# A small transpose moved from the DMA crossbar to TensorE, with a new order of all operations

## Chip, cores and metric

One core of one Trainium2 chip. The metric is the device time of one execution in microseconds (us). For this program on one core a run is called slow when it is over 1.5% above the fastest run of the same kernel, and fast otherwise. Most such slow runs of the kernel before show the same granted clock as its fast ones (of 53 executions on five chips, from 316.2 to 335.8 us, all but four lie between 0.98 and 1.00), so the label marks how the run went, and the figures don't show another state of the chip. (They say little about the start: the clock records of these profiles begin only at 13.8 to 56.1 us, and what lies before the first record is counted as full clock.) Of the 53 executions 21 are fast (316.2 to 322.0 us, with a mean of 318.1 to 319.2 in each of the five groups) and 32 slow (321.5 to 335.8, means 326.3 to 328.7). I give two ratios for each experiment: of the fast runs, and of the means of all runs.

## The reference

Linear attention with a feature map for 8 batches and 8 heads, then a gated long convolution on its output. Cut to what matters:

```python
def phi(x):                                  # q and k: (8, 8, 576, 64)
    proj = einsum('bhsd,df->bhsf', x, w_phi)             # 128 features
    proj = proj - max(abs(proj), axis=-1, keepdims=True) # row maxima
    return concatenate([exp(proj), exp(-proj)], axis=-1)
num = phi(q) @ (phi(k)^T v);  den = phi(q) @ sum_s phi(k)
x = num / (den + 1e-6)                       # -> (8, 576, 512)
x1, x2, x3 = split(x @ w_proj, 3)
y = x1 * irfft(rfft(x2) * rfft(filter)) * x3 # over the sequence, by DFT matrices
out = y @ w_out
```

## The kernel before

The whole kernel is one list of words, the PLAN. Each word calls a method that emits one operation; an engine runs its operations in the order of the list, and so does a queue of DMA issues. GpSimd issues the loads from DRAM (it casts on the way), SyncE issues the filter loads and all transposing transfers through the DMA crossbar.

```python
for word in PLAN.split():                    # run(): "Pq,0,1@2" -> self.Pq(0, 1) in PSUM bank 2
    name, _, bank = word.partition("@")
    self.bank = int(bank) if bank else None
    f, *args = name.split(",")
    getattr(self, f)(*[int(a) if a.isdigit() else a for a in args])

def load(self, n, b):                        # q, k or v of batch b: 576 KB, GpSimd's queue
    self.nc.gpsimd.dma_start(out=self.at(n + "n", b)..., in_=self.dram[n][b]...)

def trh(self, n, b, X):                      # half a batch: qT or kT, crossbar, SyncE's queue
    self.nc.sync.dma_start_transpose(
        out=self.at(n + "T", b)[:, 9 * X:9 * X + 9, :],
        in_=self.at(n + "n", b)[:, 2 * X:2 * X + 2].rearrange("p v j d -> p (v j d)"))

def gen_fwd(self):                           # the DFT matrix; gen_fwd5 is its second part
    self.nc.sync.dma_start_transpose(out=self.at("fwd")..., in_=self.G...)

def trm(self, b):                            # row maxima of q as two bf16 parts, 128x128
    self.nc.sync.dma_start_transpose(
        out=self.at("mT", b), in_=self.at("mh", b).rearrange("p g h x -> p (g h x)"))
# ... cut: w_load (w_proj in three parts of 512 KB, GpSimd), filt_load (nine loads, SyncE),
# trx, trxt (xT, xTt by the crossbar, SyncE), Pq (features of q transposed, minus mT through
# a selecting matmul), X1, X2, X3 (the projections with w_proj), H, F (DFT of filter and x2) ...
```

## Time and profile before

| | us |
|---|---|
| median of the three timed runs | 327.88 |
| lowest to highest of them | 326.14 to 329.03 |
| span of the core in the profile, an execution of 318.73 us | 317.0 |

In the lines of the profile PE is TensorE, PEld its weight load, DVE VectorE, ACT ScalarE, POOL GpSimd and SP SyncE; a q behind the name means that the engine's sequencer issues or waits, and L684 is a line of the kernel.

### The profile page before, as it was taken

The numbers are of one execution on the slowest core, as the hardware profiler recorded it, in microseconds if no ns is written. First come the engines' busy times: TensorE is split into PE (matmuls) and PEld (weight loads), VectorE is DVE, ScalarE is ACT, GpSimd is POOL, SyncE is SP. The second block draws the span as 40 slices with busy tenths as digits, with TensorE's granted clock in tenths as the row PEclk, the third lists the DMA queues.
The fourth block names the chain that finished last, engine by engine and source line by source line (L and its number), as shares of the span: only waits on it lengthen the run. The fifth ranks groups of instructions, "written<-read, shape, count | busy, mean of one in ns | idle before, by whom it ended". The sixth has DMA issues, their size and how long they took to land.

```text
span 317.0 us, 9411 instructions
## 1 busy us (share of the span) xinstructions
PE 278.9 (88%) x3901; PEld 161.2 (51%) x3901; DVE 250.7 (79%) x415; ACT 230.4 (73%) x363; POOL 220.5 (70%) x171
## 2 busy tenths in 40 slices
PE   0653478899999999999799999999999999999991
PEld 0433265546675556466355545654565554654440
DVE  6994459999988888888689898987898866786750
ACT  4794378989888888886778867788768877635542
POOL 8697914799988786698589868956688566813230
PEclk9955559999999999999999999999999999999998
DMA  6999995899889996999979949565338311360346
GB/s 123 239 211 186 223 218 82 125 155 166 143 125 179 174 144 110 205 71 132 217 147 147 164 70 205 103 116 136 78 54 125 82 35 25 70 118 2 78 95 159
DMA packets 78666, 41.50 MB, mean 131 GB/s; under 512 B 58976, under 2 KB 73440, under 8 KB 78624
## 3 DMA queue, kind: packets, MB, share of 16 engines
q1 hardware_dynamic: 63808, 24.66, 45.4%
q0 software_dynamic: 14816, 16.25, 34.6%
q8 instruction: 30, 0.49, 0.6%
q14 instruction: 12, 0.10, 0.1%
HBM read 33.75 MB, written 9.44 MB: 136 GB/s over the span
## 4 chain that ended last, share of the span: by engine, by line
PE 70%; DVE 11%; DMA 8%; ACT 3%; POOL 3%; issue 2%; SPq 1%; POOLq 0%; DVEq 0%; ACTq 0%
PE ps L844 16%; PE ps L801 9%; PE ps L895 8%; PE ps L936 8%; PE ps L458 5%; DMA out_dram<-o 5%; PE ps L709 5%; PE ps L730 4%; DMA kT<-kn 3%; DVE mq L654 3%; PE ps L587 2%; PE ps L851 2%; PE ps L594 2%; PE ps L615 2%; PE ps L621 2%
## 5 line engine op out<-in xcount | busy, mean ns | idle before, releaser
L844 PE MATMUL ps<-xT,wproj 128*128 128x512 bf16 x256 | 64.1, 379 | 0.2 <-DVE mq L654 0.2
L913 POOL TENSOR_TENSOR yT<-cv,x1s 128x576 bf16<-128x576 f32 x27 | 34.3, 1279 | 31.2 <-DVE cv L903 14.0
L654 DVE TENSOR_REDUCE mq<-ps 128x8 f32<-128x1024 f32 (+1 forms) x40 | 43.8, 1111 | 7.7 <-PE ps L594 6.7
L654 DVE TENSOR_REDUCE mk<-ps 128x8 f32<-128x1024 f32 (+1 forms) x40 | 44.2, 1112 | 3.6 <-PE ps L587 1.4
L694 POOL TENSOR_TENSOR vp<-vn,vp 128x1152 bf16<-128x1152 bf16 x16 | 34.5, 2154 | 9.2 <-ACT vp L688 7.1
L638 ACT ACTIVATE Ekm<-ps 128x1024 bf16<-128x1024 f32 x32 | 32.6, 1026 | 9.7 <-PE ps L587 5.9
L694 POOL TENSOR_TENSOR vm<-vn,vm 128x1152 bf16<-128x1152 bf16 x16 | 34.4, 2151 | 7.3 <-ACT vm L688 7.3
L936 PE MATMUL ps<-wout,yT 128*128 128x512 bf16 x144 | 36.2, 379 | 0.1
L638 ACT ACTIVATE Eqm<-ps 128x1024 bf16<-128x1024 f32 x32 | 32.7, 1025 | 4.9 <-PE ps L621 4.7
L832 POOL TENSOR_TENSOR t<-C,B 128x1024 bf16<-128x1024 bf16 x13 | 27.5, 2120 | 12.5 <-ACT C L714 9.4
L895 PE MATMUL ps<-inv,Y 128*128 128x288 bf16 (+1 forms) x192 | 36.0, 289 | 0.0
L638 ACT ACTIVATE Ekp<-ps 128x1024 bf16<-128x1024 f32 x32 | 32.9, 1028 | 3.7 <-DVE mk L654 2.2
L638 ACT ACTIVATE Eqp<-ps 128x1024 bf16<-128x1024 f32 x32 | 32.7, 1025 | 3.5 <-PE ps L621 2.8
L844 PEld LDWEIGHTS <-wproj 128*128 128x128 bf16 x256 | 23.1, 98 | 23.1 <-issue 0.2
L801 PE MATMUL ps<-wproj,eo 128*128 128x512 bf16 x128 | 31.1, 379 | 0.6 <-DVE KVs L716 0.6
L903 DVE TENSOR_TENSOR cv<-es,ps 128x288 f32<-128x288 f32 x64 | 26.5, 448 | 6.0 <-PE ps L895 4.1
L837 POOL TENSOR_TENSOR Y<-Y,t 128x1024 bf16<-128x1024 bf16 x14 | 29.6, 2125 | 2.3 <-DVE Y L827 1.1
L827 DVE TENSOR_TENSOR Y<-ps,A 128x1024 bf16<-128x1024 f32 (+1 forms) x24 | 24.7, 1042 | 4.6 <-PE ps L458 2.1
L714 ACT COPY o<-ps 128x512 f32<-128x512 f32 x29 | 17.0, 591 | 12.3 <-PE ps L936 7.6
L881 DVE TENSOR_TENSOR x1s<-ps,x1s 128x512 bf16<-128x512 f32 x32 | 21.7, 686 | 5.1 <-PE ps L844 4.7
L895 PEld LDWEIGHTS <-Y 128*128 128x128 bf16 (+1 forms) x192 | 14.4, 96 | 18.3 <-issue 9.7
L714 ACT CAST x1s<-ps 128x512 bf16<-128x512 f32 (+1 forms) x30 | 16.6, 552 | 9.6 <-PE ps L844 7.9
(153 smaller groups left out, 635.3 us busy)
## 6 DMA issues: line engine op xcount, KB each, us to landing
out_dram<-o SPq DMA_DIRECT2D x72, 128.0 KB, 2.4
vn<-in_v_dram POOLq DMA_DIRECT2D x8, 576.0 KB, 9.9
kn<-in_k_dram POOLq DMA_DIRECT2D x7, 576.0 KB, 10.0
qn<-in_q_dram POOLq DMA_DIRECT2D x7, 576.0 KB, 8.6
wproj<-in_moe_w_proj_dram POOLq DMA_DIRECT2D x3, 512.0 KB, 9.2
fl<-in_moe_filter_fft_dram SPq DMA_DIRECT2D x18, 64.0 KB, 5.0
kn<-in_k_dram POOLq DMA_DIRECT2D x2, 288.0 KB, 5.8
qn<-in_q_dram POOLq DMA_DIRECT2D x2, 288.0 KB, 8.1
```

Of the source, the lines that this page charges most:

```text
L638: self.nc.scalar.activation(e, self.db(), AF.Exp, bias=0.0, scale=1.0 if g == "p" else -1.0)
L654: self.nc.vector.tensor_reduce(out=out, in_=src, axis=AX.X, op=ALU.max, apply_absolute_value=True)
L694: self.port(eng, self.elem(eng).tensor_tensor(out=t[:, :, :, 0:64], in0=self.at("vn", b)[:, 2 * X:2 * X + 2], in1=t[:, :, :, 64:65].to_bro ...
L714: self.nc.scalar.copy(dst, src)
L801: self.mm(self.pb(0), eo[:, kt, 128 * c:128 * c + 128], w[:, kt, 512:1024], start=(kt == 0), stop=(kt == 3))
L832: self.port(eng, self.elem(eng).tensor_tensor(out=self.at("t2", b)[:, t, :], in0=self.at("C", b)[:, o, :], in1=self.at("B"), op=ALU.mult))
L837: self.port(eng, self.elem(eng).tensor_tensor(out=Y, in0=Y, in1=self.at("t2", b)[:, i:i + 3:2, :], op=ALU.add if i else ALU.subtract))
L844: self.mm(self.pb(0), w[:, kt, f0 + 128 * m:f0 + 128 * m + 128], x[:, kt, :], start=(kt == 0), stop=(kt == 3))
L895: self.mm(self.pb(0, 0, 288), y, t, start=(k == 0), stop=(k == 2))
L903: self.nc.vector.tensor_tensor(out=self.at("cv", 4 * b + m)[:, :, odd, :], in0=e, in1=o, op=ALU.subtract if odd else ALU.add)
L913: self.port(eng, self.elem(eng).tensor_tensor(out=self.at("yT", b)[:, m, 0:SEQ], in0=self.at("cv", 4 * b + m).rearrange("p j h t -> p (j h ...
L936: self.mm(self.pb(0), y[:, kt, 128 * j:128 * j + 128], w[:, kt, :], start=first and kt == ks[0], stop=last and kt == ks[-1])
```

## The change

The intent: take eight crossbar transfers out of a shared in-order queue, let TensorE transpose the 128x128 tile with the identity matrix it already has, copy it out of PSUM, and order all operations anew around that. The operations proper:

```diff
-    def trm(self, b):
-        self.nc.sync.dma_start_transpose(
-            out=self.at("mT", b), in_=self.at("mh", b).rearrange("p g h x -> p (g h x)"))
+    def Tm(self, b):
+        self.nc.tensor.transpose(self.turned(1), self.at("mh", b).rearrange("p g h x -> p (g h x)"),
+                                 self.at("ident"))
+    def Tme(self, eng, b):
+        self.copy(eng, self.at("mT", b), self.turned(1))
```

The rest of the diff is the PLAN, of which every line changes. Cut to the DMA issues between the first loads and the first projection X1 of batch 0, with marks where work of PE stands:

```
before: load v0 | nine fl | load k1 | load q1 | nine fl | trh k1,0 | trh q1,1 | trh q1,0 |
        w_proj 1 | trm 0 | (Pq 0) | fwd | trh k1,1 | fwd5 | load k2 | trh k2,1 | trh k2,0 | trx 0,0 |
        load v1 | trx 0,1 | w_proj 0 | trx 0,3 | load q2 | trm 1 | trx 0,2 | trxt 0 | load q3 |
        trh q2,0 | w_proj 2 | (X1 0) ... trh q2,1 | load k3 ... load v2
after:  load q1 | load k1 | nine fl | trh q1,0 | trh q1,1 | trh k1,0 | nine fl | load v0 | trh k1,1 |
        fwd | fwd5 | load k2 | (Tm 0, Pq 0) | trh k2,1 | trh k2,0 | w_proj 0 | trx 0,0 | trx 0,1 |
        load q2 | trh q2,0 | trh q2,1 | load v1 | trx 0,3 | w_proj 2 | trx 0,2 | w_proj 1 | trxt 0 |
        load k3 | load v2 | trx 1,0 | trh k3,1 | (X1 0) ...
```

Load and w_proj issues stand on GpSimd's queue, all others on SyncE's. Besides this some copies change engines.

## The prediction

> **What bounds the kernel now.** The core ran 317.0 us in the profile, with a mean granted TensorE clock of 0.947, in the fast state; the timed runs have a median of 327.88 us. I take the difference of some 10 us between profiled and timed runs as constant and work in profile time. I read first the page's shares and slices, to see which engine is full and where.
>
> ```profile
> PE 278.9 (88%) x3901; PEld 161.2 (51%) x3901; DVE 250.7 (79%) x415; ACT 230.4 (73%) x363; POOL 220.5 (70%) x171
> ...
> PE   0653478899999999999799999999999999999991
> ...
> PEclk9955559999999999999999999999999999999998
> ```
>
> PE is the fullest engine, but 88% is an average of two stages: slices 0 to 6 are poor, from slice 8 on all but one are full. Second, the busy times in three stretches, columns PE, PEld, DVE, ACT, POOL, clock, DMA share, GB/s.
>
> ```profile
> 0.00:60.00 60.00, 31.24 (x558) 22.94 (x558) 44.38 (x85) 40.46 (x59) 40.50 (x49) 0.74 1.01 177
> 60.00:310.00 250.00, 247.31 (x3344) 138.25 (x3343) 206.31 (x331) 188.73 (x303) 180.04 (x123) 1.00 0.76 119
> 310.00:317.00 7.00, 0.38 (x2) 0.00 (x0) 0.00 (x0) 1.17 (x2) 0.00 (x0) 0.80 0.65 151
> ```
>
> PE is idle 28.8 us before 60 us, 2.7 us in the 250 us after it, and 6.6 us in the tail. So a better order can win nearly nothing in the middle; what is to be had is at the start, and perhaps a microsecond in the tail. Third, the waits of PE, to see what the start waits for (microseconds, times, longest).
>
> ```profile
> PE ps L568 <- DMA kn<-in_k_dram: 10.1, 1, 10.1
> PE ps L587 <- DMA kT<-kn: 4.9, 1, 4.9
> PE ps L594 <- DMA qT<-qn: 4.7, 1, 4.7
> PE ps L568 <- ACT Ekp L638: 1.7, 1, 1.7
> PE ps L601 <- DMA kT<-kn: 1.4, 1, 1.4
> ...
> PE ps L621 <- DMA mT<-mh: 0.5, 1, 0.5
> ```
>
> The first 10.1 us are the first load and stay. Then come the crossbar transposes of batch 1 (kT, qT). The transfer that the change removes (mT) shows only 0.5 us. That figure hides its lateness, because an in-order engine is charged only for the wait that ends last. The SyncE queue of the start shows it (start, length, instruction).
>
> ```profile
> 20.59 1.34 SPq L548 DMA_TRANSPOSE kT<-kn  x1
> 23.43 8.37 SPq L548 DMA_TRANSPOSE qT<-qn  x2
> 31.89 1.18 SPq L683 DMA_TRANSPOSE mT<-mh  x1
> 33.17 2.16 SPq L400 DMA_TRANSPOSE fwd<-G  x1
> 35.38 3.80 SPq L548 DMA_TRANSPOSE kT<-kn  x1
> ```
>
> The source mh of batch 0 is done at 26.4 us (the timeline of VectorE: 26.19 plus 0.20). Its transfer stands in the queue behind two qT transposes and is issued at 31.89, and the first matmul that reads mT starts at 38.06. That is 11.7 us for a tile of 32 KB. Likewise the second half of kT of batch 1 is issued at 35.38 and lands 8.94 us later, a piece of the chain of waits by itself. Between 20 and 50 us VectorE is busy for 17.55 us of 30, ScalarE for 17.07: 12.5 us of VectorE time are lost there.
>
> **What the Trainium skill says.** (1) "TensorE: Matmul & The Clock Gate", Part 1: a TensorE that is not kept busy runs at half clock, and full clock comes after a few microseconds of sustained work. The trace agrees: granted clock 0.50 from 20 to 40 us, and eight Pk matmuls take 0.61 us there against 0.40 at 50.73. (2) The same page, Part 4: a PE-mode transpose of 128x128 bf16 takes about 275 ns in a kernel and lands in PSUM, so a copy follows. The trace has 18 of them from qn at a mean of 293 ns, at a part of which the clock was half. (3) "DMA: Bandwidth & Descriptors", section "Issuing engines are not separate DMA queues": all DMAs interleave on the same 16 engines. The trace agrees: mT lands 2.2 us after issue at best, 3.4 in the median and 7.6 at worst, and the DMA share between 20 and 50 us is 1.22. (4) "Perfetto Trace Analysis", "Identifying the Most-Contended Engine": matmul busy share is no good measure of the distance to the peak. I therefore checked the middle by spacing: four 512-column matmuls take 0.86 us in the chain, 0.216 each, and summing all groups at such spacings gives by my estimate about 243 us of array work in the 250. So even with hidden bubbles the middle holds perhaps 7 us, and a new order will not get all of that.
>
> **The change, part by part.** I counted both lists of operations. They are the same but for eight trm, which become eight Tm and eight Tme (5 on VectorE, 3 on ScalarE), and for the engines of some copies and products.
> - *Removed:* eight crossbar transfers, 1.18 us each of the SyncE queue, 9.4 us in all, none on the path in the middle: there PE never waited for mT. At the start the one of batch 0 cost the delay above.
> - *Added:* eight transposes on PE. At full clock one occupies the array for about 0.06 us (four 128-column matmuls in the time of a 512-column one, 0.216/4), so 0.5 us in all, on the bounding engine. Eight small copies: 0.215 us on VectorE (the row of 128x128 copies to qT), 0.27 to 0.30 on ScalarE, some 1.9 us in all, hidden in the middle.
> - *Engines moved:* weighting the moved copies and products by their rows, VectorE gains 4.5 us (with its Tme), GpSimd loses 3.2, ScalarE stays. VectorE was 83% busy in the middle and would be 84%: not a bound.
> - *New order of the start.* q comes first, q and k of batch 1 are loaded before v of batch 0, their transposes go ahead of the fwd ones, and Tm of batch 0 stands right behind its maxima. I walked the in-order lists of the start with the durations of the trace. VectorE: the angle work ends at 12.6 us as before; then copies of kT and qT, five maxq, one maxk and small work bring mlo to about 20.7, and Tme of batch 0 comes at about 24.7. So Pq of batch 0 can start at 25 in place of 36.9. Going on through batch 1 (ten maxima, 1.22 us or 0.68 each), the xn, the five filter evictions and the two folds, VectorE reaches the first X1 and X2 evictions at about 51 us if it never waits; ScalarE's walk gives 52, GpSimd's vs and filter folds let NE of batch 1 go at 48. Before, the first X1 matmul is at 60.9 us. About the same PE work precedes it in both lists, so time saved up to there is time saved at the end: at most some 10 us.
> - *Waits that stay:* the loads share the DMA engines as before, and a crossbar transpose landed 7 to 10 us after issue in that stretch. The kT of batch 1, second half, stands behind nine filter loads in the new queue; I expect it at 36 to 38 us, about when its matmuls are due. I give 3.5 us of the 10 back for that and for dependent chains at half clock (the KV group took 2.1 us there, against 1.15 later).
>
> Sum: -10 + 3.5 at the start, +0.5 for transposes, -1 to +2 in middle and tail, taken as -0.5: about -6.5 to -7, so 310.2 in the profile and about 321 timed.
>
> **The rivals.** *The wait moves.* Loads stay the limit of the start (the DMA engines move 199 GB/s from 20 to 50 us at a share of 1.22), and PE then waits for kT, qT or v of batch 1 instead of mT. For it: the kT and qT waits, 11 us together, are larger than mT's. Against it: in the old order q of batch 1 was loaded only from 14.5 us, behind v and k, and the DMA share falls to 0.45 between 50 and 60, so there is slack. This makes it 325 to 328. *The middle gives it back.* The new order has its own stalls at buffers, like the 1.8 us that PE lost between 150 and 160 in the old one, and starts loads earlier into a DMA share that is 1.17 from 100 to 150. For it: output transfers already delayed ScalarE by 4.7 us. Against it: PE lost only 2.7 us in 250. This makes it 323 to 327, slower only if several stalls come together. *The full gain.* The start is as good as the walk and a few bubbles vanish: 315 to 317.
>
> **Range and chances.** The middle case is 321.0 us. The bar of 2% is 321.3, so the main case lies right on it. The full gain pulls below, the first two rivals above, and all of them need only one wait in the start to differ. A list of operations that was newly made as a whole was presumably kept because it was better, which tips me slightly to the fast side. Range 315 to 327; faster 0.53, within 2% 0.42, slower 0.05.
>
> **What would show it.** Right: first mT matmul (Pq) near 25 to 28 us; first X1 matmul at 52 to 56; VectorE busy over 22 us between 20 and 50; PE idle before 60 us down from 28.8 to about 22; full clock granted before 45; after that PE idle still under 4 us to the end. Wrong: a wait of PE of over 5 us for kT, qT or vn of batch 1, first X1 at 59 or later (rival one); or more than 6 us of PE idle after the first X1 (rival two). The whole would be wrong if Tm itself made PE wait in each batch for mh, which would show as PE waits with releaser mh at its line.

## More of the kernel before

What the argument needs besides: the busy times by stretch (columns: stretch, its length, then PE, weight load, VectorE, ScalarE, GpSimd busy with the number of instructions, granted clock, DMA share, GB/s).

```profile
0.00:30.00 30.00, 11.62 (x186) 8.97 (x188) 23.32 (x50) 19.63 (x31) 23.07 (x35) 0.79 1.08 189
30.00:60.00 30.00, 19.62 (x381) 13.96 (x375) 21.06 (x35) 20.83 (x29) 17.43 (x15) 0.70 0.95 165
60.00:90.00 30.00, 29.45 (x485) 17.47 (x484) 28.35 (x41) 25.91 (x41) 27.79 (x19) 1.00 0.98 146
```

PE is idle 29.3 us before 90 us. And the DMA issues (number, KB of each, median us from issue to landing):

```profile
wproj<-in_moe_w_proj_dram POOLq DMA_DIRECT2D x3, 512.0 KB, 9.2
kT<-kn SPq DMA_TRANSPOSE x14, 5.2
fwd<-G SPq DMA_TRANSPOSE x2, 7.0
```

## The result, and the profile after

The kernel after ran 338.84, 339.26, 343.58 and 348.00 us: a median of 341.42 against 328.45 of the kernel before (four runs). A ratio is computed as the mean time of one kernel's fast runs over that of the other's of the same rounds, so it is not quite the ratio of these medians: 1.0378, with a 95% interval of 1.0255 to 1.0501. It is slower. In five more rounds later (run e5) it was 1.0574 (1.0375 to 1.0773). The prediction was wrong.

The profiled span grew from 317.0 to 337.5 us. These are executions of 318.73 and 339.26 us; the timed runs of before have a mean of 328.2, so some 9 of the 20.5 us are the distance between its fast and its slow executions and not the change. The same three stretches of the kernel after:

```profile
0.00:30.00 30.00, 13.49 (x154) 10.00 (x155) 25.33 (x56) 22.56 (x34) 18.94 (x33) 1.00 1.08 178
30.00:60.00 30.00, 11.44 (x305) 9.11 (x301) 15.20 (x23) 17.00 (x24) 22.81 (x18) 0.79 1.31 135
60.00:90.00 30.00, 20.19 (x290) 10.53 (x295) 14.99 (x25) 12.15 (x19) 6.23 (x7) 0.70 1.07 134
```

The first 30 us are better than before for PE, VectorE and ScalarE. From 30 to 90 us all three fall far behind. PE is idle 44.9 us before 90 us, 15.6 more than before. The other 4.9 of the 20.5 us come later: 2.7 us of idle and 2.2 us more of PE's busy time. So the loss sits in the start, with the reserve that slow executions of before may have part of it too (none was profiled; e1 and e6 below come nearest). The transpose that was added is not it: it runs early and short (start, length, and in brackets what PE had waited for).

```profile
24.61 0.26 PE L684 MATMUL banks<-ident,mh 128*128 128x128 bf16 x1 [2.79 <-DVE mk L655]
```

The first matmul on mT starts at 26.09 us, where it started at 38.06 before. What PE waits for instead (us in all, times, longest):

```profile
PE banks L443 <- DMA fwd<-G: 14.4, 1, 14.4
...
PE banks L588 <- DMA kT<-kn: 6.5, 2, 6.2
PE banks L848 <- DMA xT<-xn: 3.1, 1, 3.1
PE banks L684 <- DVE mk L655: 2.8, 1, 2.8
```

The crossbar transfers fwd, kT and xT are late. SyncE's queue shows how (start, length of the issue, instruction), to be read beside the lines of the same queue in the prediction:

```profile
32.80 1.95 SPq L549 DMA_TRANSPOSE kT<-kn  x1
34.86 7.44 SPq L401 DMA_TRANSPOSE fwd<-G  x1
42.41 12.03 SPq L406 DMA_TRANSPOSE fwd<-G  x1
54.62 14.33 SPq L549 DMA_TRANSPOSE kT<-kn  x2
69.03 3.74 SPq L772 DMA_TRANSPOSE xT<-xn  x2
```

Single issues take 7 and 12 us, where the two fwd issues took 2.16 and 2.22 before, and everything behind them waits: xT of batch 0 is issued at 69 us, where it was 46.7 before. The Trainium skill tells what such a length is: "Perfetto Trace Analysis", "Per-instruction lifecycle", says that the profiled window of such a DMA covers waiting for the descriptor generator, its work and a semaphore push, but not the movement of the data. So a window of 12.03 us, where the same transfer had 2.22 before, shows that the issue itself was held up; the trace agrees in that the transfer ahead of it, the first part of fwd, landed only at 58.7 us. The DMA issues of the kernel after:

```profile
wproj<-in_moe_w_proj_dram POOLq DMA_DIRECT2D x3, 512.0 KB, 21.4
...
kT<-kn SPq DMA_TRANSPOSE x14, 4.7
...
fwd<-G SPq DMA_TRANSPOSE x2, 23.6
```

kT is even a little better in the median of the whole run; it is the few transfers of the start that suffer. And the chain of waits has these as its long pieces:

```profile
32.80 13.89 DMA kT<-kn
...
54.62 7.94 SPq L549
62.65 12.48 DMA kT<-kn
```

What were the DMA engines doing? First a stretch of before, then two of after:

```profile
40.00:50.00 10.00, 8.13 (x173) 6.46 (x169) 6.27 (x11) 7.08 (x10) 2.15 (x1) 0.60 1.16 186
```

```profile
40.00:50.00 10.00, 3.84 (x57) 2.73 (x56) 3.46 (x8) 2.83 (x4) 5.07 (x5) 0.69 1.41 86
50.00:60.00 10.00, 1.00 (x18) 0.66 (x14) 3.22 (x5) 5.24 (x9) 7.91 (x5) 0.67 1.35 109
```

Their share is higher (1.41 against 1.16) and they move half as much (86 GB/s against 186). They are not short of work, each packet takes longer on average. Packets of the trace by their start, counted by me:

```
                 256 bytes (transposing)     1024 and 1152 bytes (loads)
before 40-50     4765 of mean 24 ns          512 of mean 109 ns
after  40-50     1954 of mean 89 ns          344 of mean 145 ns
after  50-60     1300 of mean 84 ns          720 of mean 140 ns
```

I call this the crawl below.

### The profile page after: what moved, and what is told of

Read it like the earlier page. It is cut to its first block, busy times and chain, and to the rows that moved or that the text cites.

```text
span 337.5 us, 9400 instructions
## 1 busy us (share of the span) xinstructions
PE 281.1 (83%) x3866; PEld 161.4 (48%) x3909; DVE 256.4 (76%) x424; ACT 231.0 (68%) x365; POOL 218.0 (65%) x168
## 4 chain that ended last, share of the span: by engine, by line
PE 69%; DMA 13%; SPq 7%; DVE 3%; POOL 3%; issue 2%; ACT 1%; DVEq 0%; POOLq 0%; ACTq 0%
PE banks L848 16%; PE banks L805 9%; PE banks L899 8%; DMA kT<-kn 8%; PE banks L940 8%; PE banks L459 6%; SPq L549 6%; PE banks L713 5%; PE banks L734 4%; DMA qn<-in_q_dram 2%; PE banks L855 2%; PE banks L588 2%; PE banks L616 2%; PE banks L595 2%; DMA fl<-in_moe_filter_fft_dram 1%
## 5 line engine op out<-in xcount | busy, mean ns | idle before, releaser
L848 PE MATMUL banks<-xT,wproj 128*128 128x512 bf16 x239 | 62.2, 379 | 5.7 <-DMA xT<-xn 3.1
L917 POOL TENSOR_TENSOR yT<-cv,x1s 128x576 bf16<-128x576 f32 x23 | 29.3, 1279 | 32.0 <-DVE cv L907 16.1
L655 DVE TENSOR_REDUCE mq<-banks 128x8 f32<-128x1024 f32 (+1 forms) x40 | 43.9, 1113 | 7.5 <-PE banks L595 5.7
L655 DVE TENSOR_REDUCE mk<-banks 128x8 f32<-128x1024 f32 (+1 forms) x40 | 44.0, 1111 | 1.8 <-PE banks L602 0.8
L639 ACT ACTIVATE Eqp<-banks 128x1024 bf16<-128x1024 f32 x32 | 32.5, 1023 | 17.3 <-PE banks L622 17.1
L639 ACT ACTIVATE Ekp<-banks 128x1024 bf16<-128x1024 f32 x32 | 32.8, 1029 | 8.3 <-PE banks L588 8.1
L848 PEld LDWEIGHTS <-wproj 128*128 128x128 bf16 x256 | 23.6, 98 | 28.7 <-issue 4.9
L639 ACT ACTIVATE Ekm<-banks 128x1024 bf16<-128x1024 f32 x32 | 33.0, 1033 | 5.5 <-PE banks L588 4.2
L639 ACT ACTIVATE Eqm<-banks 128x1024 bf16<-128x1024 f32 x32 | 32.5, 1025 | 6.2 <-PE banks L622 5.3
L940 PE MATMUL banks<-wout,yT 128*128 128x512 bf16 x136 | 35.6, 379 | 1.1 <-DVE yT L917 0.4
L899 PE MATMUL banks<-inv,Y 128*128 128x288 bf16 (+1 forms) x192 | 34.8, 289 | 0.0
L805 PE MATMUL banks<-wproj,eo 128*128 128x512 bf16 x117 | 31.6, 392 | 0.8 <-DVE eo L789 0.2
```

The lines of the kernel that those rows point to most:

```text
L639: self.nc.scalar.activation(e, self.db(), AF.Exp, bias=0.0, scale=1.0 if g == "p" else -1.0)
L655: self.nc.vector.tensor_reduce(out=out, in_=src, axis=AX.X, op=ALU.max, apply_absolute_value=True)
L805: self.mm(self.pb(0), eo[:, kt, 128 * c:128 * c + 128], w[:, kt, 512:1024], start=(kt == 0), stop=(kt == 3))
L848: self.mm(self.pb(0), w[:, kt, f0 + 128 * m:f0 + 128 * m + 128], x[:, kt, :], start=(kt == 0), stop=(kt == 3))
L899: self.mm(self.pb(0, 0, 288), y, t, start=(k == 0), stop=(k == 2))
L917: self.port(eng, self.elem(eng).tensor_tensor(out=self.at("yT", b)[:, m, 0:SEQ], in0=self.at("cv", 4 * b + m).rearrange("p j h t -> p (j h ...
```

## The experiments

Two theories. **Theory O**: the new order asks DMA work of the start in another sequence (two w_proj loads back to back, filter loads between transposing transfers, later batches' loads earlier), transposing transfers crawl beside it, and PE waits for them. **Theory T**: the eight transposes on PE and their copies cost the time themselves. Single executions scatter by some 2% either way, so most runs have five rounds. Kernels of one group ran on one chip beside the kernel before. The record calls the change itself slower, and every experiment for which it gives a verdict unclear (its bar is 2%); the ratios below are evidence of different strength, not verdicts.

| run | edit | median us | before, median | ratio, fast runs (95%) | ratio of all means | PE idle before 90 us |
|---|---|---|---|---|---|---|
| before / after | | 328.45 / 341.42 | | 1.0378 (1.0255 to 1.0501) | | 29.3 / 44.9 |
| e1 | before, only the transposes on PE | 331.4 | 325.4 | none | 1.019 | 39.9 |
| e2 | after, crossbar transposes kept | 332.9 | 325.4 | 1.0344 (1.0171 to 1.0516) | 1.037 | 40.6 |
| e3 | after, filter loads together | 332.5 | 325.4 | 1.0266 (0.992 to 1.061) | 1.025 | 32.3 |
| e4 | after, w_proj part 2 later | 333.6 | 325.4 | none | 1.033 | 36.4 |
| e5 | after, unedited | 341.6 | 322.4 | 1.0574 (1.0375 to 1.0773) | 1.058 | 42.0 |
| e6 | as e1 | 328.6 | 322.4 | 1.0136 (0.999 to 1.0282) | 1.015 | 35.8 |
| e7 | after, three DMA places mended | 331.3 | 322.4 | 1.0412 (1.0317 to 1.0508) | 1.026 | 35.5 |
| e8 | after, q and k of batch 1 by PE | 335.4 | 322.4 | 1.0304 (1.0137 to 1.0471) | 1.042 | 30.8 |
| e9 | before, three DMA places of after | 328.6 | 324.4 | 1.0291 (1.0222 to 1.0359) | 1.014 | 39.1 |
| e10 | e7, two loads later | 328.3 | 324.4 | none | 1.010 | 27.7 |
| e11 | after, fwd earlier (flawed) | 333.9 | 324.4 | 1.0451 (1.0389 to 1.0512) | 1.030 | 39.3 |
| e12 | e10 and e8's edit | 330.5 | 324.4 | 1.0361 (1.028 to 1.0442) | 1.021 | 33.7 |
| e13 | after, fwd ahead of kT | 330.7 | 321.5 | 1.0313 (1.02 to 1.0426) | 1.021 | 31.6 |
| e14 | e10, crossbar transposes back | 334.7 | 321.5 | 1.0457 (1.0359 to 1.0554) | 1.034 | 34.3 |
| e15 | before, w_proj part 2 earlier | 328.6 | 321.5 | 1.0295 (1.0221 to 1.037) | 1.018 | 34.9 |
| e16 | before, k3, v2, qT of batch 2 earlier | 324.5 | 321.5 | 1.0046 (0.9898 to 1.0194) | 1.005 | 30.7 |
| e17 | before, w_proj part 0 later | 326.8 | 323.6 | 1.022 (1.0114 to 1.0327) | 1.008 | 30.6 |
| e18 | e10, two loads spread | 323.2 | 323.6 | 1.0136 (1.009 to 1.0183) | 0.998 | 29.8 |

Chips: e1 to e4 on one, e5 to e8, e9 to e12, e13 to e16, and e17 and e18 on one each. "None" means that too few runs counted as fast for an interval. The last column is from the one profiled run, which fell among the slower runs of its kernel in e1, e5 and e6.

### The two halves of the change alone (e1, e6, e2)

e1 and e6: the order of before, each crossbar transfer of the maxima replaced by a transpose and a copy.

```diff
- mlo,DVE,0 trm,0 Qn,1,3@0 ... ex,k,p,1,0@6
+ mlo,DVE,0 Qn,1,3@0 ... ex,k,p,1,0@6 Tm,0@4 Tme,DVE,0@4        (likewise for the other batches)
```

> The order of before with only the eight crossbar transfers of mh replaced by transposes on TensorE and copies. Theory O (the new order is what costs: between 40 and 72 us the DMA engines crawl and PE waits 14.4 us for the fwd transfer): this run is as before or faster, 319 to 330 us timed, ratio to before 0.97 to 1.005, since Pq of batch 0 no longer waits until 38 us. Rival T (the transposes and copies themselves cost): this run is near the changed kernel, ratio 1.02 or more.

> The order of before with only the transfers of mh replaced by transposes on TensorE: the same kernel as the first run, whose executions scattered from 320 to 340 us. Theory O (the order costs): mean ratio to before 0.985 to 1.015. Theory T (the transposes and copies cost): 1.02 or more.

e2: the order of after, with the crossbar transfer right behind the operation that makes its source.

```diff
- Tm,0@0 Tme,DVE,0@0                     (and the other seven pairs)
+ trm,0                                  (behind mlo of its batch)
```

> The new order with the crossbar transfers of mh kept (each right behind the low part of mh), no transpose on TensorE. Theory O: as the changed kernel or slower, ratio to before 1.03 to 1.06, with the same crawl of the DMA engines. Rival T: near before, ratio 0.98 to 1.01.

e1 gave 320.4 to 339.6 us in four runs; e6 says 1.4% with an interval from just no difference to 2.8%. So in the old order T may hold for up to that much. e2 has no transpose on PE at all and is 3.4% slower, so the new order can cost that without them. But the crawl that I expected in it didn't come: its fwd landed at 43.1 and 45.3 us, and PE waited for mT, 20.1 us in all, the longest 13.3. The kernel after has that wait no longer, and is not faster than e2: the time it gained there it lost to fwd and kT.

The profiles of e1 and e6, both of slow executions (335.9 and 327.0 us), show something else. Their loads stand where before has them (w_proj at 30.7 us, q2 at 36.5), and fwd is late all the same: it lands at 52.5 and 54.7 us in e1, at 46.9 and 51.2 in e6, against 40.2 and 46.3 in the fast execution of before. Issues of e6, and its stretch from 40 to 50 us:

```profile
31.95 4.63 SPq L401 DMA_TRANSPOSE fwd<-G  x1
41.94 7.19 SPq L406 DMA_TRANSPOSE fwd<-G  x1
```

```profile
40.00:50.00 10.00, 3.53 (x46) 2.51 (x46) 3.36 (x5) 4.51 (x5) 0.00 (x0) 0.95 1.31 160
```

So a milder crawl comes in the old order too, with no load moved. Whether it marks the slow executions of before, or came with the transposes, no run settles.

### Undoing DMA places in the kernel after (e3, e4, e7, e8)

e3 and e4, one edit each; e7 has both and moves the qT transposes of batch 2 as well; e8 takes load off the crossbar in another way.

```diff
e3:  - ... Pk,0,1@4 filt_load,SP,1 ...              + filt_load,SP,0 filt_load,SP,1 ...
e4:  - trx,0,3 w_load,proj,2 NE,0,2@2               + load,v,2 w_load,proj,2 rc,1,0@6
e7:  both, and  - load,q,2 trh,q,2,0 ... trh,q,2,1  + trxt,0 trh,q,2,0 trh,q,2,1
e8:  - trh,q,1,0 trh,q,1,1 trh,k,1,0 trh,k,1,1      + T and Te of q and k of batch 1 on PE
```

> The changed kernel with its second nine filter loads issued at once behind the first nine, ahead of all crossbar transposes, as in before. Theory O-a (the crawl comes from direct loads on the SyncE queue that stand between crossbar transposes while the other queue is full): the crawl goes, fwd lands by 45 us, the ratio to before falls to 0.96 to 0.99. Theory O-b (two loads of w_proj queued together start it): no change, 1.03 to 1.05.

> The changed kernel with the load of the third part of w_proj issued behind the load of v of batch 2, some 20 us later, so that no two loads of w_proj are queued together. Theory O-b: the crawl goes or is halved, ratio to before 0.96 to 1.01. Theory O-a: no change, 1.03 to 1.05.

> The changed kernel itself, unedited, so that it and the edits of this call are measured on one chip, with five rounds against the scatter of single executions that the first four runs showed. Both theories expect a ratio to before of 1.03 to 1.05 and PE idle of 38 to 46 us in the first 90 us of its profile.

> The changed kernel with three edits to its start that take DMA work out of the way: the second nine filter loads right behind the first nine, the third part of w_proj loaded behind v of batch 2, and the transposes of q of batch 2 behind the xT transfers of batch 0 on the SyncE queue. Theory O in its refined form (the new order asks for more DMA work at the start than the DMA engines deliver, and urgent crossbar transfers stand behind it): ratio to the changed kernel 0.95 to 0.98, ratio to before 0.98 to 1.01. Theory T: as the changed kernel, 1.03 to 1.05.

> The changed kernel with q and k of batch 1 transposed by TensorE, as those of batch 0 are, in place of four crossbar transfers. It adds 36 transposes and eight copies, some 3 us of work each for PE and for the copying engines, and takes four crossbar transfers out of the crowded stretch. Theory O refined: the first use of q and k of batch 1 follows their loads, the fwd transfer lands 8 us or more earlier, ratio to the changed kernel 0.95 to 0.98. Theory T: slower by 1 to 3 us, as transposes are added.

e5 repeats the kernel after unedited: 1.0574, the wait for fwd again 15.5 us. Against it e7's fast runs are at 0.985 (1.0412/1.0574), its means at 0.970: its worst run (334.0 us) equals the best of e5 (333.9). e3, e4 and e8 point the same way, with wider scatter. None comes to the level of before, as e3, e4 and e7 had been expected to (e4 and e7 put w_proj part 2 right behind the load of v2, 0.8 us apart); in e7 PE waited 9.1 us for xT, beside which the loads of k3, v2 and w_proj part 2 were issued within 4 us. That gave the next step.

### The opposite direction: the kernel before with places of the kernel after (e9, e15, e16)

e9 moves three groups of DMA issues, e15 and e16 two of these alone. Order of engine work and crossbar transposes are those of before.

```diff
e15: - ex,q,p,1,1@2 w_load,proj,2 Pk,2,0@4          + w_load,proj,0 w_load,proj,2 maxqt,1@0
e16: - ... load,k,3 ... load,v,2 ... trh,q,2,*      + trh,q,2,0 trh,q,2,1 trx,0,2 ... trxt,0 load,k,3
                                                    + NE,1,0@6 load,v,2
e9:  both, and  - filt_load,SP,0 em,m,0,0           + trh,k,1,0 filt_load,SP,0
```

> The kernel before (crossbar transposes of the maxima kept, its own order of all work on the engines), with only the places of some DMA issues taken from the kernel after: the second nine filter loads behind the first kT transpose of batch 1, w_proj part 2 right behind part 0, the loads of k of batch 3 and v of batch 2 before the first projections of batch 0 instead of behind them, and the qT transposes of batch 2 ahead of the last xT transpose of batch 0. Theory O (the new order's placing of DMA work costs the time): 2 to 4% slower than the kernel before, ratio 1.02 to 1.04, TensorE idle in the first 90 us 35 to 45 us instead of 29.3, and long waits for kT, fwd or xT. Theory T (the transposes and copies of the maxima cost it): ratio 0.99 to 1.01, as this kernel has none of them. A third possibility, that the order of work on the engines and not of the DMA issues costs it: also about 1.00.

> The kernel before, with the load of w_proj part 2 moved right behind that of part 0, nothing else. Theory O by the w_proj loads: 1.01 to 1.03 of the kernel before, and a slow transfer of fwd, kT or xT beside them. If another of the three moved groups did it: 0.99 to 1.01.

> The kernel before, with the loads of k of batch 3 and v of batch 2 ahead of the first projections of batch 0 and the qT transposes of batch 2 ahead of its last xT transpose, nothing else. Theory O by these: 1.01 to 1.03, a late xT. If another group did it: 0.99 to 1.01.

One load of 512 KB, moved from behind the first transposes of x to right behind another load, costs 2.95% by fast runs and 1.8% by means, as much as all three groups together; e16 shows no clear difference (-1.0 to 1.9%). So the place of a DMA issue alone can cost time, as theory O says, and theory T has no part in it, since none of these kernels has a transpose that before has not. How large the cost is depends on the ratio: the six runs of e15 (326.8 to 332.1 us) and of e9 (327.6 to 330.5) all lie among or just above the slow runs of before in their groups (321.5 to 330.7, and 324.4 to 335.8), and none among the fast ones. The moved load may thus bring about each time what happens to before in 32 of its 53 executions; the profile of e6 above, with the load unmoved, looks like that of e15. The 2.9% of e9 are not the whole 3.8 to 5.7% of the kernel after, which has a second pair of loads beside its transposing transfers (q2 with v1) and another order on SyncE's queue. SyncE's queue in e15:

```profile
33.15 3.71 SPq L400 DMA_TRANSPOSE fwd<-G  x1
36.91 9.09 SPq L548 DMA_TRANSPOSE kT<-kn  x1
46.09 3.73 SPq L405 DMA_TRANSPOSE fwd<-G  x1
```

The loads are issued at 30.7 and 31.5 us, where before issued one at 30.7 and the other at 59.6. The first fwd transfer lands at 49.8 us instead of 40.2, kT at 50.7 instead of 44.3, and the first X1 matmul starts at 67.2 instead of 60.8. The DMA engines in the stretch where before moved 186 GB/s:

```profile
40.00:50.00 10.00, 4.14 (x54) 2.97 (x53) 3.04 (x4) 5.71 (x6) 0.56 (x1) 1.00 1.30 170
```

Share up, throughput down. The clock is not the cause: the 1.00 is no reading, as this trace has no clock record before 55.0 us, but the 512-column matmuls on qT (L615) between 36 and 44 us take 0.58 to 0.63 us here and 0.58 to 0.61 in before, against 0.37 to 0.39 later in both. The bytes do not explain it either. By my estimate from the packets, a part of w_proj is 512 packets of 1024 bytes, 32 for each of 16 engines, at the 97 ns that they took in before: 3.1 us. The delay of fwd is 9.5.

### The place of fwd in the queue (e11, e13)

e11 was to issue fwd ahead of the kT transpose, and I placed it wrongly: fwd5 went ahead of the copies that fill its source.

```diff
e11: - trh,k,1,1 gen_fwd gen_five gen_fwd5          + gen_fwd gen_fwd5 trh,k,1,1 gen_five
e13: - trh,k,1,1 gen_fwd gen_five gen_fwd5          + gen_fwd gen_five gen_fwd5 trh,k,1,1
```

> The kernel after with the two transposing transfers of the DFT matrix issued ahead of the second kT transpose of batch 1 on the same queue, nothing else. If the 14 us wait for fwd comes from its place in the in-order queue: fwd lands by 50 us, TensorE's wait for it falls below 5 us, and the time falls by 1 to 3%. If it comes from DMA engines that crawl whatever is asked of them first: the wait moves to kT or xT and the time stays within 1% of the kernel after, 1.04 to 1.055 of the kernel before.

> The kernel after with the kT transpose of the second half of batch 1 issued behind the two transposing transfers of the DFT matrix instead of ahead of them, with the copies that fill the second one's source kept ahead of it (the run e11 had them behind it, so that it transposed a source not yet filled and VectorE waited 15 us for it). If the place of fwd in the in-order queue cost the 14 us wait: TensorE's wait for fwd under 5 us, the time 1 to 3% below that of the kernel after, ratio to the kernel before 1.02 to 1.04. If the DMA engines are slow whatever is first: the wait goes to kT, and the ratio stays 1.04 to 1.06.

In e11 VectorE's copies had to wait until the transfer had read their destination:

```profile
DVE G L396 <- DMA fwd<-G: 15.0, 1, 15.0
```

so a wait of the start was swapped for another, and the run says nothing on the queue (its output has a part of the DFT matrix from an unfilled source; the comparison with the reference did not notice, so it is not sharp there). One thing can be read from it: with all of GpSimd's loads of that stretch held back too, fwd landed 3.3 us after issue. e13 is the clean one: 1.0313 against 1.0574 of e5 on another chip. The wait for fwd is gone, one of 9.9 us for kT takes its place (us, times, longest):

```profile
PE banks L588 <- DMA kT<-kn: 9.9, 1, 9.9
```

Its two w_proj loads are still back to back (37.1 and 37.9 us), and fwd lands at 42.6 and 50.6 us instead of 58.7 and 65.7. So the place in the queue decides what waits. How much of the loss it accounts for stays open: the ratio fell from 1.0574 (e5) or 1.0378 (first rounds), each beside before in rounds of its own, and that makes it a sixth to a half by fast runs.

### Is the new order good once its loads are moved? (e10, e12, e14)

e10: e7 with the loads of k3 and v2 behind the first projections. e12: that with e8's edit. e14: e10 with the crossbar transposes of the maxima back.

```diff
e10: - load,k,3 ex,k,p,1,3@6 ... load,v,2 w_load,proj,2 ... trh,k,3,1 maxkt,2@0
     + X2,0,0@0 load,k,3 load,v,2 ... trh,k,3,1 trh,q,3,1
e14: - Tm,b Tme,b                                   + trm,b behind mlo of its batch
```

> The kernel after with all the DMA placements that I suspect undone: filter loads together, w_proj part 2 later, qT transposes of batch 2 behind the last xT transpose of batch 0 (these three are the earlier mended kernel, 1.026 by means), and now the loads of k of batch 3 and v of batch 2, with the kT transpose that needs the first, behind the first projections of batch 0. Theory O: ratio to the kernel before 0.98 to 1.01, TensorE waits for xT under 4 us, idle in the first 90 us 27 to 32 us. If the engine order itself costs the rest: it stays at 1.02 to 1.03. Theory T: about 1.03 too.

> The mended order of the run above it but one, and besides it q and k of batch 1 transposed by TensorE instead of four crossbar transfers. Theory O: the start is freer still, ratio to the kernel before 0.97 to 1.00, TensorE idle in the first 90 us 24 to 30 us. If the engine order or the transposes themselves cost the time: 1.02 or more.

> The mended order of e10 (1.010 of the kernel before by means), with the eight crossbar transfers of the row maxima in place of TensorE's transposes and their copies, each right behind the operation that makes its source. If the transposes on TensorE are a gain, as the change intended: this is slower than e10, ratio to the kernel before 1.015 to 1.035, TensorE waiting for mT for some us in all. If theory T holds (the transposes and copies cost): faster than e10, 0.99 to 1.005. If neither matters: 1.00 to 1.015.

e10 is 1.010 of before by means; its one fast run, the profiled one, took 320.91 us. Its start is what the prediction wanted of the change: first X1 matmul at 55.4 us, PE idle 23.3 us before 60 us. Some of it is given back between 60 and 90 us, 4.4 us of idle where before had 0.6. The two profiles from 0 to 90 us, first e10, then e14:

```profile
0.00:90.00 90.00, 62.31 (x1049) 41.31 (x1058) 73.80 (x128) 68.33 (x100) 62.61 (x66) 0.96 1.13 180
```

```profile
0.00:90.00 90.00, 55.71 (x952) 36.75 (x953) 67.72 (x117) 62.85 (x92) 52.92 (x59) 0.94 1.05 161
```

e14 is worse by 6.6 us of PE there, and PE's waits have a line for it that e10 lacks:

```profile
PE banks L621 <- DMA mT<-mh: 15.8, 3, 8.4
```

The profile of e10 is of its fastest run, 7 us under the next, so part of the 6.6 us may be scatter; the 15.8 us of waits for mT are not in e10 at all. The two runs were on two chips, so each is compared with the kernel before on its own. In this order, which was made for it, the transpose on PE is a gain of 2 to 3% (1.034/1.010 by means, 1.041/1.012 by medians): the opposite of theory T. e12, which I had expected to be best, is slower than e10: its fwd took 18.0 us to land in the median against 11.9, and the DMA engines moved 106 GB/s at a share of 1.40 from 30 to 60 us. So fewer crossbar transfers do not by themselves end the crawl.

### Fewer loads beside the transposing transfers (e17, e18)

```diff
e17 (before): - w_load,proj,0 maxqt,1@0             + filt_fold,POOL,1 w_load,proj,0
e18 (e10):    - trx,0,1 load,q,2 ... w_load,proj,1  + trx,0,2 load,q,2 ... trxt,0 w_load,proj,1
```

> The kernel before, with the load of w_proj part 0, which it issues at 30.7 us beside the transfers of mT, fwd and kT, moved behind the last of GpSimd's filter folds, some 9 us later (about 40 us), nothing else. If a load beside those transfers is what delays them: fwd lands at 36 to 38 us instead of 40.2 and 46.3 for its second part, ratio to the kernel before 0.98 to 0.995. If there is slack, or if the moved load delays xT instead: 0.995 to 1.01.

> The mended order of e10, with the load of q of batch 2, issued at 29.8 us beside the transfers of kT and fwd, moved to about 37 us, and the load of w_proj part 1, that was there, moved to about 48 us. If loads beside those transfers delay them: fwd lands some 4 us earlier than in e10 (42.0 and 46.5), ratio to the kernel before 0.98 to 1.00, and it beats both kernels. If not: 1.00 to 1.015, as e10.

e17 missed: it is slower by fast runs (1.022), and by means no faster (1.008). Its first fwd transfer landed at 37.3 us as expected, but the moved load was now issued 3.3 us behind another, and the second one landed at 50.9 instead of 46.3. e18 has its loads one by one, and is level with before by means (0.998; medians 323.2 and 323.6) and 1.4% slower by fast runs; its six runs spread over 6 us, those of before over 17. It does not beat before. The loads in that stretch and the landing of the two fwd transfers, from the traces:

| run | GpSimd's loads, issued at (us) | fwd lands at | PE idle before 90 us |
|---|---|---|---|
| before | w_proj 30.7; q2 36.5 | 40.2, 46.3 | 29.3 |
| e16 | w_proj 30.6; q2 36.4 | 40.2, 46.3 | 30.7 |
| e6 (slow) | w_proj 30.7; q2 36.5 | 46.9, 51.2 | 35.8 |
| e1 (slow) | w_proj 30.7; q2 36.5 | 52.5, 54.7 | 39.9 |
| e15 | w_proj 30.7 and 31.5; q2 37.2 | 49.8, 51.9 | 34.9 |
| e17 | q2 35.5 and w_proj 38.8 | 37.3, 50.9 | 30.6 |
| after | q2 29.9 and v1 30.7; w_proj 36.0 and 36.8 | 58.7, 65.7 | 44.9 |
| e10 | q2 29.8 and v1 30.6; w_proj 37.3 | 42.0, 46.6 | 27.7 |
| e18 | v1 30.7; q2 38.3 | 40.8, 41.8 | 29.8 |

Two loads issued close together go with a late fwd transfer in e15, e17 and the kernel after, but not in e10, and e1 and e6 have it late without such a pair. So the pair is neither needed nor enough. What is shown by times is less: that the loads' places matter (e15 by its one load, e7 against e5 by three edits of DMA issues alone, 3.0% by means), and that the same engine order with other DMA places comes close to before (e10 1.010 and e18 0.998 by means). What starts the crawl is not shown.

## Why the prediction was wrong

- *What it started from.* It took the 10 us between the profile (317.0) and the timed runs (327.88) as constant. They are not: the profiled execution itself took 318.73 us, 1.7 above its span, and was a fast one. So its 310.2 us of profile would be about 312 us timed, by my estimate from that offset, and 321 mixes a fast execution with slower ones.
- *What bounds the kernel.* Right: the middle was full before and stayed so (PE idle between 90 and 300 us: 2.0 us before, 4.4 after). Everything was decided in the start.
- *Removed and added.* Right in kind. PE waited 2.8 us once for the source of Tm, and the first matmul on mT ran 12 us earlier. The moved work came out near the forecast: VectorE 5.7 us busier (4.5 foreseen), GpSimd 2.5 less (3.2). e14 shows that the removed wait was worth having in the new order.
- *New order of the start.* First mT matmul predicted near 25 to 28 us, measured 26.1: right. VectorE busy over 22 us between 20 and 50: 8.94, 8.53 and 3.46, so 20.9, all lost after 40. First X1 at 52 to 56: measured 76.5. The walk of the engines was sound as long as DMA kept up: e10 and e18, with the same order of engine work, start X1 at 55.4 and 56.7.
- *Waits that stay.* This is the step that failed. It said that the kT of batch 1, second half, would land at 36 to 38 us, and gave 3.5 of the 10 us back. That kT landed at 46.7, fwd at 58.7 and 65.7, and the kT of batch 2 after 72. With the walk's 51 us for X1 and the measured 76.5, the term of 3.5 us was some 25 us. I had walked the lists of the engines and not those of the two DMA queues; I looked at one transfer, and took its delay from a trace in which one w_proj load was beside it, where the new order puts two loads and then two more.
- *The rivals.* The first, that the wait moves, was the mechanism, and its signs came: a kT wait of over 5 us, X1 after 59. It expected 325 to 328 us, because I let the new wait at most undo the gain. What I had against it, that the DMA share fell to 0.45 between 50 and 60 us, was a property of the old order. The second, stalls in the middle, has 2.7 us of idle after 90 us.
- *Chances.* "Kept because it was better" was no reason; slower had 0.05.

What stays open: why a transposing transfer's packets take up to 3.7 times as long (89 ns against 24). The Trainium skill, "DMA: Bandwidth & Descriptors", section "SWDGE vs HWDGE vs iDMA", says that GpSimd's and SyncE's DMAs feed different queues inside each DMA engine, and that the engine goes round between them. By that, if it takes turns packet by packet as the trace counts them (no run here shows this), a load packet of 106 ns between two transposing packets of 18 ns (medians of before) would stretch a transfer as long as a load is in flight, and no longer: the estimate of 3.1 us above. It fits in kind, and falls short of the 9.5 us measured in e15. No run here separates the packets' own slowness from the engines getting out of step (in the kernel after the first w_proj load of the pair landed on its first engine at 44.7 us, on half of them by 54.6). Nor is it settled why before itself spreads from 316 to 336 us; the same signs show in its trace between 130 and 150 us (a share of 1.33 and 1.39 at 116 and 114 GB/s), where PE stays full.

## What to carry to other kernels

When a change reorders a kernel whose start is bound by DMA, walk the DMA queues like engines, load by load, before crediting time that the engines could save: here one 512 KB load moved next to another cost 1.8% by means of all runs, 2.95% by fast runs. Look for a high DMA share with few GB/s, and for issue windows that grow from 2 to 12 us; they name the stretch and the queue. Look which execution a profile caught before its time is compared with another's: here before's was one of its fast ones. And judge a replaced operation in both orders: the same transpose on PE was no gain in the old order (1.4% slower by fast runs, within the scatter) and a gain of 2 to 3% in the mended new one.

## What the Trainium skill lacked or had wrong

- "DMA: Bandwidth & Descriptors", section "Rules for kernel authors", says that a transpose next to ordinary DMAs needs nothing. For correctness no run here contradicts it. It does not say what it can cost: from before to after, with GpSimd's loads in flight in both, transposing packets between 40 and 50 us went from a mean of 24 ns to 89, the core's DMA from 186 GB/s to 86 at a higher share, and the landing of fwd from 7.0 us to 23.6.
- The same page, "Issuing engines are not separate DMA queues", says that DMAs of all issuers interleave on the same 16 engines. The traces agree. It does not say what the order of the issues can be worth: moving one 512 KB load (e15) cost 1.8% by means and 2.95% by fast runs, and fwd landed 9.5 us later in its profile, three times what the load's packets explain (an estimate of 3.1 us).
- "Perfetto Trace Analysis", "Per-instruction lifecycle", names what the window of such a DMA issue covers, but gives no sizes: here 2.16 and 2.22 us for the two fwd issues of before, 7.44 and 12.03 us for those of after.
- I found no page that says that single executions of a DMA-bound start scatter: 316.2 to 335.8 us for one kernel, 21 of 53 up to 322.0.
